# A gated unit on one core: the first half's down products as seven block products, with the weight combinations made during its up products

## The chip, the cores and the metric

The kernel runs on one core of a Trainium2 chip. The time of an execution is the device time of that core in microseconds (us). TensorE is called PE here, VectorE DVE, ScalarE ACT, GpSimd POOL; SP is the engine that issues most transfers.

## What is computed

The input x has 2048 tokens of 640 features. Two blocks follow one another, each with a layer norm that is shifted and scaled by values made from c (adaLN), and a residual. The first block is a state-space convolution over the tokens, made with Fourier transforms. The second is a bilinear gated unit with 1536 hidden features:

```python
h = _layernorm(x) * (1 + cb) + sb
g = h @ w_gate                  # 2048 x 640 by 640 x 1536
u = h @ w_up
y = (g * u) @ w_down            # 2048 x 1536 by 1536 x 640
x = x + gb * y
```

All is in float32. Each matrix product is made as three: every operand is split into a high part, rounded to the type that PE takes, and the rest, the low part; then high by high, low by high and high by low are added.

## The kernel before

The convolution takes the first 500 us and the change does not touch it. The gated unit works on two halves of the tokens. A half is two blocks of 512 tokens, T = 0 and 1, held with the features on the partitions. The hidden features are 12 groups of 128 (NF = 12); f counts them within a half, i = 12 * half + f over both.

**Gate and up products.** They are made as seven block products over the two token blocks and combinations of the weights. `x_1` and `x_2` make one of the seven, from the split gate weights `WS[i]` that `split_g` prepares; for f from 2 to 8 they run three groups ahead. `y_1`, `z_1`, `y_2`, `z_2`, `y_3` add the other six in two banks of PSUM. Between them ACT and DVE read a bank (`s`, `z`), and DVE multiplies at the end of `y_3`: `h` and `a` are the products of gate and up for the two blocks. A bank that is read in the middle goes on being added to: `y_3` must wait until DVE has read `z`. `sums_u` makes sums of raw weights, `split_u` splits them. All products of the two halves' x, y and z have 512 columns.

**Down products, second half.** `down` makes them as seven block products (Winograd's form of Strassen's scheme), over two halves of the hidden features and two halves of the 640 output columns (DC = 320). Product j runs over six chunks c; m = 6j + c counts the 42 chunks. `d_sum` makes the sums of activations, `d_prep` splits them into `AH[m]`, five chunks ahead. The weight combinations lie, already split, in the DRAM tensor `wdc`; `w_load(q)` brings chunks 2q and 2q + 1 of it through POOL's queue into one of four `wsg` buffers, so that load q waits for the chunks of load q - 4. `post` adds finished products to the residual rows. Products 0, 2, 4, 6 add up in four banks (`ACC["A"]`), products 1 and then 3, 5 in four others (`ACC["C"]`).

**The weight combinations.** `fold` scales the rows of the down weights by gb on POOL and writes them to the DRAM tensor `wdg`, during the first half's up products. During the second half's up products, at steps listed in `FOLD`, `f_load` reads a third of it, `f_sum` makes four sums on DVE, `f_hi` the seven high parts on ACT and `f_lo` the seven low parts on DVE, and both write them to `wdc`.

**Down products, first half.** `plain` makes them for one token block after the other without block products: 12 groups, four rows of 128 tokens, three products, each row of 640 columns in pieces of 384 and 256. `p_prep` splits activations and weights, the latter from `wdg`. Between its groups `LATER` puts the preparation of the second half.

**Order.** It is written out by hand: what the program calls first stands first in an engine's queue, and every engine works its queue in order. Split gate weights are kept in the DRAM tensor `wsd` for the second half.

Of the kernel before, what the change touches and what calls it, by code (L numbers as in the profile page):

```python
# [224 lines left out]
def tile_kernel(ctx: ExitStack, tc: tile.TileContext, I, out):  # L225
# [768 lines left out]
    PAIRS = [("g", 2 * p) for p in range(NF // 2)] + [("d", T, 2 * p) for T in range(2) for p in range(NF // 2)]  # L994
    NP = len(PAIRS)

    def raw():

        t = mk(f"wga{(NP - len(PAIRS)) % 2}", [P, 2 * D])
        k = PAIRS.pop(0)  # L1000
        f = k[-1]
        if k[0] == "g":
            t = t.rearrange("p (k m) -> p k m", k=NB)
            SY.dma_start(t, wv[0][:, :, f * P : f * P + 2 * P])
            w = [t[:, :, j * P : j * P + P] for j in range(2)]
        else:
            t = t.rearrange("p (k m) -> p k m", k=2)
            SY.dma_start(t, wdg[:, f : f + 2, :])
            w = [t[:, j] for j in range(2)]
        for j in range(2):  # L1010
            WR[(*k[:-1], f + j)] = w[j]

    def used(f):
        if f % 2 and PAIRS:
            raw()
# [15 lines left out]
    def split_g(i):  # L1031
        t = wsg()
        WS[i] = tuple(t[:, j].rearrange("p (k m) -> p k m", k=NB) for j in range(2))
        if i >= NF:
            G.dma_start(t, wsd[:, i - NF])
# [72 lines left out]
    def x_1(i):  # L1108
        UX[i] = UA[i] = pa(i % 5)
        prod(UX[i], [(WS[i], k, HX[0], k) for k in (0, 1)], last=False)  # L1110
        x_e(i)
# [217 lines left out]
    for t in range(3 * NK + 24):  # L1329
# [17 lines left out]
        if t == 3 * NK + 1:  # L1347
# [5 lines left out]
            wdg = dram1.tile([P, NF, D], F32, name="wdg")  # L1353
            wsd = dram1.tile([P, NF, 2, D], F32, name="wsd")
# [115 lines left out]
    AP, WD2, AC, BP = {}, {}, {}, {}  # L1470

    def p_prep(tb, f):
        w = WR.pop(("d", tb, f))
        t = wsg()
        WD2[tb, f] = t[:, 0], t[:, 1]
        m = tb * NF + f
        if m < 2:
            AP[tb, f] = tuple(mk("e", [P, 512], F32, 4).bitcast(F32R) for _ in range(2))
        else:
            if m in (2, 21):  # L1480
                n, k = ((SX, 9), (H2, 3))[m > 2]
                BP[0] = tuple(mk(x, [P, k, 512], F32R) for x in n)
            AP[tb, f] = tuple(h[:, (m - 2) % 9 if m < 21 else m - 21] for h in BP[0])
        hilo(*AP[tb, f], AT[NF * tb + f])
        hilo(*WD2[tb, f], w)
        used(f)

    C0 = 384

    def plain(tb, f):  # L1490
        if f == 0:
            b = [pa(j) for j in (2, 3, 4, 0, 1, 5)]
            c1 = [b[j].rearrange("p (t d) -> p t d", t=2)[:, :, : D - C0] for j in (2, 5)]
            AC[tb] = [(b[j][:, :C0], c1[t // 2][:, t % 2]) for t, j in enumerate((0, 1, 3, 4))]
        (ah, al), (dh, dl) = AP.pop((tb, f)), WD2.pop((tb, f))
        for t in range(4):
            ts = slice(t * P, t * P + P)
            for n, (x, w) in enumerate(((ah, dh), (al, dh), (ah, dl))):
                for c in range(2):
                    cs = slice(0, C0) if c == 0 else slice(C0, D)  # L1500
                    st = f == 0 and n == 0 and (c == 0 or t % 2 == 0)
                    PE.matmul(AC[tb][t][c], x[:, ts], w[:, cs], start=st, stop=f == NF - 1 and n == 2 and (c == 0 or t % 2 == 1))  # L1502

    XR = {}

    def res_l(tb, b):
        XR[tb] = mk(f"xb{b}", [P, 4, D])
        SY.dma_start(XR[tb], x2d[:, 4 * tb : 4 * tb + 4, :])

    def fin(tb):  # L1510
        for t in range(4):
            x = XR[tb][:, t, :]
            V.tensor_tensor(x[:, :C0], AC[tb][t][0], x[:, :C0], op=OP.add)
            V.tensor_tensor(x[:, C0:], AC[tb][t][1], x[:, C0:], op=OP.add)
            SY.dma_start(outv[:, 4 * tb + t, :], x)

# [26 lines left out]
    def down(half, m, last=False):  # L1543
        j, c = divmod(m, NH)
        if c == 0:
            if j == 0:
                ACC["A"] = [pa(t) for t in range(4)]
            if j in (1, 3):
                ACC["C"] = [pa(4), pa(5), pg(), pg()]
        ps = ACC["AC"[j in (1, 3, 5)]]  # L1550
        w = [WD[m // 2][:, l, c % 2 * DC : c % 2 * DC + DC] for l in range(2)]
        for t in range(4) if not last else (last - 1,):
            for n, (a, b) in enumerate(((0, 0), (1, 0), (0, 1))):
                PE.matmul(ps[t][:, :DC], AH[m][a][:, t * P : t * P + P], w[b], start=c == 0 and n == 0 and j in (0, 1, 3), stop=c == NH - 1 and n == 2, skip_group_check=True)  # L1554
# [8 lines left out]
    def post(half, j, ts=range(4), E=None):  # L1563
# [4 lines left out]
        for t in ts:  # L1568
            V.tensor_tensor(x[:, t], ps[t][:, :DC], x[:, t], op=OP.add)
# [12 lines left out]
    def tokens2(tb, T, k, dve):  # L1582

        tv = a_tile((TV0, TV1)[T] + k)
        head_t(pg() if tb > 1 else pa((0, 1, 4, 5)[k % 4]), tv, k, XB[tb][:, :, k * P : k * P + P], dve)
# [11 lines left out]
    def fold(f):  # L1597

        r, p = divmod(f - 1, 3)
        if f > 9:  # L1600
            if f == 10:
                head_l(2)
            return
        if f and p == 0:
            FT[9] = mk("xb0", [P, 4, D])
            SY.dma_start(FT[9], wv[2][:, 4 * r : 4 * r + 4, :])
        elif f:
            for k in range(2 * p - 2, 2 * p):
                G.tensor_tensor(FT[9][:, k], FT[9][:, k], gbr, op=OP.mult)
            if p == 2:  # L1610
                SY.dma_start(wdg[:, 4 * r : 4 * r + 4, :], FT[9])
# [33 lines left out]
    FOLD = {n: [] for n in range(80)}  # L1645
    for r in range(3):
        b = (1, 13, 25)[r]
        for n in range(4):
            FOLD[b + 1 + n // 2].append((f_sum, n))
        for j in range(7):  # L1650
            o = b + 3 + j + (max(j - 1, 0) if r == 2 else 0)
            FOLD[o].append((f_hi, r, j, j))
            FOLD[o + 1].insert(0, (f_lo, r, j))
        if r < 2:
            FOLD[b + 10].append((f_load, r + 1))

    def combos(n):
        for g_, *a_ in FOLD.get(n, ()):
            g_(*a_)

    SUMS = [(0, 4), (1, 0), (1, 1), (1, 2), (0, 5)] + [(1, c) for c in range(3, NH)] + [(2, c) for c in range(NH)]
    LATER = {(0, 1): [(stats, 2, 0)], (0, 2): [(stats, 2, 2)], (0, 3): [(head_i, 2, (0, 1))], (0, 4): [(head_i, 2, (2, 3))],
             (0, 6): [(raw_u, NF)], (0, 9): [(raw_u, NF + 1)], (1, 0): [(new_h,), (tokens2, 2, 0, 0, False)], (1, 1): [(head_l, 3), (tokens2, 2, 0, 2, False)],
             (1, 2): [(sums_u, NF), (tokens2, 2, 0, 1, False)], (1, 3): [(split_u, NF), (tokens2, 2, 0, 3, False)],
             (1, 4): [(tokens2, 2, 0, 4, False), (stats, 3, 0), (sums_u, NF + 1)], (1, 5): [(stats, 3, 2), (res_l, 1, 0)],
             (1, 6): [(head_i, 3, (0, 1))], (1, 7): [(head_i, 3, (2, 3))],
# [200 lines left out]
```

## Time and profile before

| | |
|---|---|
| Time, median of 3 runs | 987.37 us (986.79 to 993.78) |
| Profiled execution: time, span | 988.54 us, 986.8 us |
| PE busy | 889.2 us, 90% of the span |
| DVE, ACT, POOL busy | 723.8, 579.4, 509.1 us |
| Mean granted PE clock | 0.961 |
| First half's gate and up products | about 527 to 670 us |
| First half's down products | 670 to 759 us |
| Second half's gate and up products | 759 to 908 us |
| Second half's down products, end | 908 to 987 us |

The span runs from the first to the last recorded instruction; the time holds 1.7 us more. Times within the profile count from the start of the span. In a row of a timeline stand start and duration in us, the engine, the line of the kernel, the operation, its output and inputs, and in brackets how long the engine was idle before it and for what it waited. In a row of a group stand the count, the total in us and the mean in ns.

### The profile page before, as it was taken

To read this page: it belongs to the slowest core of one execution; us is meant where nothing else is said; L and a number is where in the kernel's file an instruction comes from. 1 tells how busy PE (TensorE), PEld (TensorE's weight loads), DVE (VectorE), ACT (ScalarE), POOL (GpSimd) and SP (SyncE) were. 2 spreads that over 40 slices of the span, in tenths; PEclk is the share of its full clock that TensorE was granted. 3 is DMA by queue.
4 is the path that set the end of the run, shared out by engine and by line. 5 is a ranking of instruction groups with operands and counts; after the bars stand their busy time and mean duration, and the time that the engine had idled before them with its cause. 6 is when DMAs were issued, how large, how long until landed. Compare 5 with 4: busy or idle time off the path is not lost.

```text
span 986.8 us, 26765 instructions
## 1 busy us (share of the span) xinstructions
PE 889.2 (90%) x11134; PEld 720.2 (73%) x11134; DVE 723.8 (73%) x1400; ACT 579.4 (59%) x1076; POOL 509.1 (52%) x400
## 2 busy tenths in 40 slices
PE   4867898799789789988879999999999999999998
PEld 3565556586476557667736888889999788888998
DVE  8789568888978888794857665457676756578952
ACT  4869989987888887863336333334355443435430
POOL 5978899699879979960030354440113122222110
PEclk9877979999989889999999999999999999999999
DMA  7746654556246534658595665733564676658875
GB/s 254 262 142 223 204 194 147 172 165 185 77 153 181 152 105 126 205 172 257 189 273 191 222 191 182 242 125 113 184 217 124 197 231 222 222 179 292 237 244 187
DMA packets 158817, 188.54 MB, mean 191 GB/s; under 512 B 9828, under 2 KB 128360, under 8 KB 157544
## 3 DMA queue, kind: packets, MB, share of 16 engines
q1 hardware_dynamic: 149480, 155.51, 49.4%
q0 software_dynamic: 4752, 21.63, 7.6%
q10 hardware_dynamic: 4464, 9.70, 2.6%
q8 instruction: 87, 1.43, 0.6%
q14 instruction: 34, 0.28, 0.1%
HBM read 124.22 MB, written 62.59 MB: 189 GB/s over the span
## 4 chain that ended last, share of the span: by engine, by line
PE 55%; DVE 14%; ACT 12%; issue 10%; POOL 4%; DMA 3%; SPq 0%; DVEq 0%; POOLq 0%; ACTq 0%
PE pa L1078 18%; PE psg L1078 9%; PE pa L1502 9%; PE psfc L893 2%; PE kg L826 2%; PE kg L811 2%; PE psfa L893 2%; PE psfb L893 2%; ACT trb L230 1%; ACT tra L230 1%; PE psfc L950 1%; POOL EQ L714 1%; PE psfb L950 1%; PE pa L1554 1%; ACT L230 1%
## 5 line engine op out<-in xcount | busy, mean ns | idle before, releaser
L1055 POOL TENSOR_TENSOR tf<-wur,wgb 128x256 f32<-128x256 f32 x23 | 17.8, 775 | 246.9 <-DVE wtl L1026 199.5
L714 POOL TENSOR_TENSOR EQ<-LQ,RH 128x1536 f32<-128x1536 f32 x40 | 124.1, 3104 | 9.7 <-DVE QtB L771 9.5
L1026 DVE TENSOR_TENSOR wtl<-tf,wth 128x256 fp32r<-128x256 f32 (+1 forms) x72 | 36.7, 513 | 59.7 <-ACT wth L230 59.7
L714 POOL TENSOR_TENSOR Phb<-LH,DH 128x1536 int32<-128x1536 int32 x20 | 62.2, 3112 | 13.9 <-ACT tra L230 13.9
L714 POOL TENSOR_TENSOR EP<-LP,RH 128x768 f32<-128x768 f32 x40 | 66.0, 1650 | 0.0
L714 POOL TENSOR_TENSOR Pha<-LH,DH 128x1536 int32<-128x1536 int32 (+1 forms) x21 | 62.4, 2971 | 2.3 <-ACT trb L230 2.0
L1502 PE MATMUL pa<-wsg,sh 128*128 128x384 f32 (+1 forms) x304 | 58.4, 311 | 0.0
L826 PE MATMUL kg<-QtB,PtB 64*32 64x64 f32 x2560 | 48.7, 229 | 5.8 <-DVE QtB L770 5.3
L826 PEld LDWEIGHTS kg<-QtB,PtB 64*32 64x32 f32 x2560 | 41.7, 114 | 16.1 <-issue 7.2
L1502 PEld LDWEIGHTS pa<-wsg,sh 128*128 128x128 f32 x304 | 45.7, 189 | 0.0
L1541 POOL DMA_DIRECT2D wsg<-wdc x21 | 11.2, 531 | 66.5 <-PE pa L1554 35.6
L1026 DVE TENSOR_TENSOR wsg<-wga,wsg 128x640 fp32r<-128x640 f32 x36 | 33.7, 943 | 13.8 <-ACT wsg L230 13.8
L230 ACT ACTIVATE sh<-a 128x512 fp32r<-128x512 f32 x55 | 33.3, 625 | 13.9 <-PE psg L1554 6.2
L230 ACT ACTIVATE wsg<-wga 128x640 fp32r<-128x640 f32 x36 | 26.1, 730 | 25.0 <-PE pa L1502 12.8
L1026 DVE TENSOR_TENSOR sl<-a,sh 128x512 fp32r<-128x512 f32 x55 | 37.5, 702 | 4.0 <-ACT sh L230 4.0
L1078 PE MATMUL pa<-hh,wsg 128*128 128x512 f32 x150 | 40.2, 394 | 0.0
L1148 POOL TENSOR_SCALAR hfa<-xb,hr,hr 128x128 f32<-128x128 f32 x4 | 2.3, 577 | 67.5 <-DVE hr L283 67.5
L230 ACT ACTIVATE s<-pa 128x512 f32<-128x512 f32 x12 | 7.2, 598 | 48.5 <-PE pa L1078 48.5
L769 DVE TENSOR_TENSOR QtA<-tra,EQ 128x1024 f32<-128x1024 f32 x20 | 24.4, 1220 | 15.0 <-PE kg L811 7.0
L230 ACT ACTIVATE wth<-tf 128x256 fp32r<-128x256 f32 (+1 forms) x72 | 32.5, 481 | 4.9 <-DVE tf L1056 1.8
L230 ACT ACTIVATE a<-pa 128x512 f32<-128x512 f32 x12 | 7.2, 598 | 47.7 <-PE pa L1078 47.7
L1502 PE MATMUL pa<-wsg,sl 128*128 128x384 f32 (+1 forms) x152 | 34.4, 308 | 0.0
(656 smaller groups left out, 3125.6 us busy)
## 6 DMA issues: line engine op xcount, KB each, us to landing
wsg<-wdc POOLq DMA_DIRECT2D x21, 640.0 KB, 5.3
wgb<-B_w_gate SPq DMA_DIRECT2D x24, 320.0 KB, 4.6
wur<-B_w_up SPq DMA_DIRECT2D x24, 320.0 KB, 5.8
wsd<-wsg SPq DMA_DIRECT2D x12, 640.0 KB, 3.9
wga<-wdg SPq DMA_DIRECT2D x12, 640.0 KB, 3.9
wsg<-wsd POOLq DMA_DIRECT2D x12, 640.0 KB, 4.9
wdc<-xb SPq DMA_DIRECT2D x21, 320.0 KB, 3.3
TVb<-WD SPq DMA_DIRECT2D x22, 256.0 KB, 3.5
```

Of the source, the lines that this page charges most:

```text
L230: return S.activation(o, i, f, **kw)
L714: G.tensor_tensor(o.rearrange("p x (h l) -> p x h l", l=8), lo.unsqueeze(2).to_broadcast([P, rows, nh, 8]), hi.rearrange("p h x -> p x h") ...
L769: return [lambda: V.tensor_tensor(Qt[:, :, :, 0:32], tr[:, :, :, ::-1], e[:, :, 0:32].unsqueeze(1).to_broadcast([P, 2, R, 32]), op=OP.mult ...
L811: PE.matmul(kg[j * 32 : j * 32 + 32, dd, :], PtA[:, c, dl * 4 + j, :], QtA[:, c, dl * 4 + j, :], start=dd == 0 and c == 0, stop=False, til ...
L826: PE.matmul(kg[j * 32 : j * 32 + 32, dd, :], PtB[lo : lo + 64, c, r, :], QtB[lo : lo + 64, c, r, :], start=False, stop=dd == 7 and c == 1, ...
L893: PE.matmul(r[c][par * 64 : par * 64 + 64, i, :], t_tw[:, k0 + k, c, :], src[:, k, :], start=True, stop=True, tile_position=(0, par * 64))
L950: PE.matmul(r[par][:, i], t_ti[lo : lo + 64, qd * 4 + i, c, :], x[lo : lo + 64, c, i, :], start=c == 0, stop=c == 1, tile_position=(lo, 0))
L1026: V.tensor_tensor(lo, v, hi, op=OP.subtract)
L1055: E.tensor_tensor(t[:, 0:2], u[:, 0:2], g[:, 0:2], op=OP.subtract)
L1078: PE.matmul(ps, w[a][:, k], x[b][:, l], start=first and n == 0 and m == 0, stop=n == 2 and m == len(ks) - 1, skip_group_check=True)
L1502: PE.matmul(AC[tb][t][c], x[:, ts], w[:, cs], start=st, stop=f == NF - 1 and n == 2 and (c == 0 or t % 2 == 1))
L1541: G.dma_start(WD[q], wdc[:, q // 3, q % 3])
```

## The change

The first half's down products are made by `down`, `d_sum`, `d_prep`, `w_load` and `post`, as the second half's. `plain`, `p_prep`, `fin`, `fold`, the tensor `wdg` and `LATER` are gone. `f_load` now reads the down weights themselves and `f_gb` scales them, on POOL or DVE; this and the sums, splits and writes to `wdc` stand in the first half's steps, which `PLAN` lists. Its numbers count 3f, 3f + 1 and 3f + 2 for the three places of group f, and 36 + m for chunk m of the first half's down products. The second half's `FOLD` steps are gone. In the first half `d_sum` runs on POOL, in the second on DVE as before.

So that one bank is free for transposes, the first half's `ACC["C"]` uses three banks from product 3 on: the fourth row of tokens goes into the rests of two of them, in pieces of 192 and 128 columns. Only gate groups 0 to 3 are kept in `wsd`; 4 to 11 are loaded and split again in the second half. `SU` says for which groups `sums_u` runs on POOL; the others go to DVE.

```diff
-    PAIRS = [("g", 2 * p) for p in range(NF // 2)] + [("d", T, 2 * p) for T in range(2) for p in range(NF // 2)]
+    PAIRS = [2 * p for p in range(NF // 2)] + [2 * p for p in range(NF // 2 + 2, NF)]
...
     def split_g(i):
         t = wsg()
         WS[i] = tuple(t[:, j].rearrange("p (k m) -> p k m", k=NB) for j in range(2))
-        if i >= NF:
+        if NF <= i < NF + 4:
             G.dma_start(t, wsd[:, i - NF])
             return
         hilo(*WS[i], WR.pop(("g", i)))
         if i > 3:
-            keep(i, t)
             used(i)
...
     def down(half, m, last=False):
         j, c = divmod(m, NH)
         if c == 0:
             if j == 0:
-                ACC["A"] = [pa(t) for t in range(4)]
+                ACC["A"] = [[(pa(t), 0, 0, DC)] for t in ((0, 2, 3, 1), (1, 2, 3, 0))[half]]
             if j in (1, 3):
-                ACC["C"] = [pa(4), pa(5), pg(), pg()]
+                b = [pa(4), pg(), pg()]
+                ACC["C"] = [[(x, 0, 0, DC)] for x in b]
+                if half == 0 and j == 3:
+                    ACC["C"].append([(b[0], DC, 0, 512 - DC), (b[1], DC, 512 - DC, DC)])
+                else:
+                    ACC["C"].insert(1, [(pa(5), 0, 0, DC)])
         for t in range(4) if not last else (last - 1,):
             for n, (a, b) in enumerate(((0, 0), (1, 0), (0, 1))):
-                PE.matmul(ps[t][:, :DC], AH[m][a][:, t * P : t * P + P], w[b], ...
+                for x, o, c0, c1 in ps[t]:
+                    PE.matmul(x[:, o : o + c1 - c0], AH[m][a][:, t * P : t * P + P], w[b][:, c0:c1], ...
...
-            SY.dma_start(FT["f"][:, 2 * j : 2 * j + 2], wdg[:, 2 * r + NH * j : 2 * r + NH * j + 2, :])
+            SY.dma_start(FT["f"][:, 2 * j : 2 * j + 2], wv[2][:, 2 * r + NH * j : 2 * r + NH * j + 2, :])
+
+    def f_gb(n, E=None):
+        (E or G).tensor_tensor(FT["f"][:, n], FT["f"][:, n], gbr, op=OP.mult)
...
+    SU = ((0, 1, 2, 3, 6, 8, 10, 11), (2, 5, 6, 7, 9, 10, 11))
+    PLAN = {
+        4: [(f_gb, 1, V), (f_gb, 2), (f_gb, 3, V)],
...
+        27: [(f_load, 2), (d_sum, 0, 0), (d_sum, 0, 1)],
+        28: [(raw_u, NF), (f_gb, 0)],
...
+        36: [(d_sum, 0, 3), (xq_l, 0, 0, 0, 0), (f_hi, 2, 4, 4), (f_lo, 2, 3)],
...
+        40: [(d_sum, 1, 4), (d_sum, 1, 0), (new_x, 3), (d_sum, 1, 1), (row_l, 2, 1), (d_sum, 2, 0), (d_sum, 1, 3)],
+        41: [(d_sum, 2, 2), (d_sum, 2, 1)],
...
     def combos(n):
-        for g_, *a_ in FOLD.get(n, ()):
+        for g_, *a_ in PLAN.get(n, ()):
             g_(*a_)
...
             if f + 2 < NF:
-                sums_u(i + 2)
+                sums_u(i + 2, (V, G)[f in SU[half]])
...
-            if todo and m > 0:
+            if half and todo and m > 0:
                 d_sum(*todo.pop(0), V)
-            if j < 6:
+            if j < 6 or half == 0:
                 down(half, m)
...
+            if half == 0:
+                combos(36 + m)
+        if half == 0:
+            post(0, 6)
+            continue
```

Two pieces of the queues show what was moved. The first is DVE's, in the first half's last groups. Before, from its reading `s` of group 10 to its reading `z` of group 11 (L1441 and L1449 are the reads of `z_2` and `y_3`, L1451 is `a`, L1026 a low part):

```order
L1441 TENSOR_TENSOR a_8743<-psg,a_8743 128x512
L1449 TENSOR_TENSOR a_8797<-pa_8478,z 128x512
L1451 TENSOR_TENSOR a_8545<-a_8545,a_8743 128x512
L1026 TENSOR_TENSOR e<-a_7629,e 128x512
L1026 TENSOR_TENSOR wsg<-wga_8524,wsg 128x640
L1436 TENSOR_TENSOR z<-pa_8579,z 128x512
```

The same stretch now, with the lines of the changed kernel (L1554 is a weight sum, L1566 a low part of a combination, L1017 any other low part):

```order
L1430 TENSOR_TENSOR a_8815<-psg,a_8815 128x512
L1554 TENSOR_TENSOR xb_8741<-xb_8741 128x2x320
L1566 TENSOR_TENSOR xb_8741<-xb_8741,xb_8742 128x2x320
L1554 TENSOR_TENSOR xb_8742<-xb_8741 128x640
L1017 TENSOR_TENSOR hl_8746<-a_7628,hl_8746 128x512
L1438 TENSOR_TENSOR a_8886<-pa_8516,z 128x512
L1440 TENSOR_TENSOR a_8586<-a_8586,a_8815 128x512
L1554 TENSOR_TENSOR xb_8742<-xb_8741,xb_8742 128x640
L1566 TENSOR_TENSOR xb_8741<-xb_8741,hst 128x2x320
L1017 TENSOR_TENSOR hl_8746<-a_7629,hl_8746 128x512
L1566 TENSOR_TENSOR xb_8742<-xb_8742 128x640
L1425 TENSOR_TENSOR z<-pa_8623,z 128x512
```

Between the two reads there were four instructions; now there are ten, six of them for the weight combinations. Three gains and another sum stand just ahead of this piece, after group 9's `a`.

The second piece is POOL's, in the first half's down products. Before, POOL issued there only the loads of kept gate weights for the second half, with the second half's first token sums (L1403, L1404):

```order
L1035 DMA wsg<-wsd 128x1280
L1403 TENSOR_TENSOR a_9754<-a_9341,a_9698 128x512
L1404 TENSOR_TENSOR a_9755<-a_9381,a_9753 128x512
L1035 DMA wsg<-wsd 128x1280
L1403 TENSOR_TENSOR a_9795<-a_9426,a_9738 128x512
L1404 TENSOR_TENSOR a_9796<-a_9478,a_9794 128x512
```

Now, from the third activation sum behind the load for chunks 8 and 9 to the load for chunks 12 and 13 (L1483 is `w_load`, L1474 to L1479 are `d_sum`):

```order
L1474 TENSOR_TENSOR hh_8745<-a_8292,a_8886 128x512
L1475 TENSOR_TENSOR a_8292<-a_7632,a_8292 128x512
L1477 TENSOR_TENSOR a_7630<-hh_8745,a_7630 128x512
L1483 DMA wsg<-wdc 128x1280
L1477 TENSOR_TENSOR a_7632<-hh_8745,a_7632 128x512
L1477 TENSOR_TENSOR a_7628<-hh_8745,a_7628 128x512
L1477 TENSOR_TENSOR a_7629<-hh_8745,a_7629 128x512
L1479 TENSOR_TENSOR a_8155<-a_8155,a_7628 128x512
L1477 TENSOR_TENSOR a_7631<-hh_8745,a_7631 128x512
L1479 TENSOR_TENSOR a_8375<-a_8375,a_7630 128x512
L1479 TENSOR_TENSOR a_8267<-a_8267,a_7629 128x512
L1483 DMA wsg<-wdc 128x1280
```

Two sums stand ahead of the first row shown, behind the load before. Every load of the down stage is now in one queue with these sums, and each is issued only when those ahead of it are done.

More of the change, by code (lines that the diff above doesn't have):

```diff
@@ L1468, in d_pair @@
         return tuple(h[:, l % 9] for h in AR[l > 8])
[L1470 to L1515, printed above, removed]
     def d_prep(m):
@@ L1735, in tile_kernel @@
             split_u(2, "a")
-            fold(1)
             z_1(1)
```

192 lines of the change are left out of this document (97 added, 95 removed).

## The prediction

> **What bounds the kernel now.** I read the page's 40 slices first, then busy time by stage, then the timelines of TensorE (PE), POOL and DVE at the places the change touches. The slices show PE at 9 or more from slice 22 to the end, at a granted clock of 9 tenths or more. The windows cut that part into its four stages: first half's gate and up products, first half's down products, second half's gate and up products, second half's down products.
>
> ```profile
> PE   4867898799789789988879999999999999999998
> core 0: us, PE busy (x) PEld busy (x) DVE busy (x) ACT busy (x) POOL busy (x), PEclk, DMA share, GB/s
> 527.00:670.00 143.00, 143.00 (x628) 117.40 (x627) 86.59 (x150) 57.37 (x123) 52.81 (x52) 1.00 0.58 193
> 670.00:759.00 89.00, 89.00 (x616) 88.74 (x615) 61.47 (x136) 46.00 (x76) 14.21 (x15) 1.00 0.47 150
> 759.00:908.00 149.00, 148.60 (x649) 121.27 (x649) 100.32 (x169) 61.63 (x126) 39.56 (x54) 1.00 0.69 226
> 908.00:987.00 79.00, 74.73 (x507) 74.15 (x505) 50.84 (x91) 22.68 (x39) 8.99 (x17) 0.99 0.72 222
> ```
>
> PE is busy for all of the first two windows at clock 1.00, while DVE has 56 and 28 us free there, ACT more. So this part's length is PE's work plus what PE waits. PE's pace is read from starts, since the spans of pipelined matmuls overlap.
>
> ```profile
> 643.51 0.61 PE L1078 MATMUL pa<-sh,wth 128*128 128x512 f32 x2
> 652.35 0.61 PE L1078 MATMUL pa<-sh,wth 128*128 128x512 f32 x2
> 670.03 7.20 PE L1502 MATMUL pa<-wsg,e 128*128 128x384 f32 x48
> 677.07 0.46 PE L1502 MATMUL pa<-wsg,sh 128*128 128x384 f32 x2
> 715.79 0.60 PE L1169 MATMUL psg<-ident,xb 128*128 128x128 f32 x4
> 716.15 0.54 PE L1502 MATMUL pa<-wsg,sh 128*128 128x384 f32 x2
> 908.36 1.48 PE L1554 MATMUL pa<-wsg,hl 128*128 128x320 f32 x9
> 912.44 0.53 POOL L1541 DMA_DIRECT2D wsg<-wdc  x1 [11.71 <-PE pa L1554]
> 915.97 0.53 POOL L1541 DMA_DIRECT2D wsg<-wdc  x1 [3.00 <-PE pa L1554]
> 919.49 0.53 POOL L1541 DMA_DIRECT2D wsg<-wdc  x1 [3.00 <-PE pa L1554]
> ```
>
> The first two rows stand one late group f apart: 39 matmuls of 512 columns in 8.84 us, 226.7 ns each. The plain down products take 7.04 us for 48, 146.7 ns each (24 of 384 columns, 24 of 256). In the second half each load of a pair of down weights is released by 24 matmuls of 320 columns, and comes every 3.52 us: 146.7 ns each, 1.76 us a chunk of 12. Four transposes of 128 columns take 0.36 us, 90 ns each.
>
> **The change, part by part.** *Fewer matmuls.* Before: 2 blocks x 12 groups x 4 rows of tokens x 3 x 2 column pieces = 576 in the first half's down stage. After: 7 products x 6 chunks x 4 x 3 = 504, of which 36 (the fourth row of tokens in products 3 and 5) are cut into pieces of 192 and 128 columns: 468 of 320 columns and 72 short ones. Before 576 x 0.1467 = 84.5 us; now 468 x 0.1467 = 68.7 us and 36 pairs. A line through 512 and 320 columns (80.0 ns for 192) gives 93 ns for 192 columns and 67 for 128, so 0.160 us a pair is the least; two full 0.1467 are the most, 0.293. The transposes at 90 ns are the nearest row to the 128 piece, so I take 0.093 + 0.090 = 0.183, 6.6 us in all (5.8 to 10.6). The gain on PE is 84.5 - 68.7 - 6.6 = **9.2 us** (5.2 to 10.0). The 40 transposes, the gate and up products and all ahead of them stay.
>
> *Work that lies beside PE.* Gone from DVE and ACT: 24 splits of down weights (820 ns on DVE below) and 24 of activations; from SP and POOL the copies of gate weights 4 to 11 through wsd, and the scaled weights through wdg. New in the first half: 42 splits, and the weight combinations. These are 12 sums (L1618) and 21 low parts (L1630) on DVE, their 21 high parts on ACT; half of POOL's 12 gains go to DVE.
>
> ```profile
> L1630 DVE TENSOR_TENSOR xb<-xb 128x640 fp32r<-128x640 f32 x9 | 8.5, 948 | 0.0
> L1618 DVE TENSOR_TENSOR xb<-xb 128x640 f32<-128x640 f32 x9 | 8.0, 884 | 0.2
> L1026 DVE TENSOR_TENSOR sl<-a,sh 128x512 fp32r<-128x512 f32 x55 | 37.5, 702 | 4.0 <-ACT sh L230 4.0
> 672.04 0.82 DVE L1026 TENSOR_TENSOR wsg<-wga,wsg 128x640 fp32r<-128x640 f32 x1
> 672.77 0.69 DVE L1026 TENSOR_TENSOR sl<-a,sh 128x512 fp32r<-128x512 f32 x1
> 673.37 0.82 DVE L1026 TENSOR_TENSOR wsg<-wga,wsg 128x640 fp32r<-128x640 f32 x1
> ```
>
> About 37 us more for DVE in the first up stage (33 x 0.9, six gains at 0.8, four groups of sums from POOL, less what spills into the down stage) makes some 124 of 143: hidden on the whole. The second half loses those 33 instructions and gets 8 gate splits, so its cover grows. I cost both stages at nothing but for two places where an order is too tight; without that cover each microsecond would count in full.
>
> *Place 1, groups 9 to 11 of the first half.* These have no gate products left and last 8.84 us. PE may start the last products (y_3) of group 11 only when DVE has read its bank (z). Between DVE's two products of group 9 and that z now stand 10 instructions of 640 columns (3 gains, 4 sums, 3 low parts), 7 of 512 and group 11's split of up weights. By starts: 10 x 0.73 + 7 x 0.61 + 2.0 (split, from the rows below) = 13.6 us. PE leaves 6.80 of group 11 and 8.84 of group 10, less 1.42 for the two products: 14.2 us. It fits by 0.6, if nothing stretches it. But POOL now makes a gain and two sums at that time.
>
> ```profile
> 648.04 0.43 DVE L1026 TENSOR_TENSOR wtl<-tf,wth 128x256 fp32r<-128x256 f32 x1 [1.80 <-ACT wth L230]
> 649.08 0.42 DVE L1026 TENSOR_TENSOR wtl<-tf,wth 128x256 fp32r<-128x256 f32 x1
> 650.68 0.69 DVE L1441 TENSOR_TENSOR s<-psg,s 128x512 f32<-128x512 f32 x1
> 751.13 1.28 POOL L1404 TENSOR_TENSOR a<-a,a 128x512 f32<-128x512 f32 x1 [1.36 <-DVE a L1402]
> 752.94 1.30 POOL L1403 TENSOR_TENSOR a<-a,a 128x512 f32<-128x512 f32 x1
> 752.89 1.90 DVE L1401 TENSOR_TENSOR a<-a,a 128x512 f32<-128x512 f32 x1 [1.85 <-ACT a L230]
> 754.83 0.69 DVE L1402 TENSOR_TENSOR a<-a,a 128x512 f32<-128x512 f32 x1
> 752.35 0.57 POOL L1035 DMA_DIRECT2D wsg<-wsd  x1
> L1403 POOL TENSOR_TENSOR a<-a,a 128x512 f32<-128x512 f32 x2 | 2.6, 1294 | 1.1 <-ACT a L230 1.1
> 590.11 1.46 POOL L1055 TENSOR_TENSOR tf<-wur,wgb 128x256 f32<-128x256 f32 x1 [5.47 <-DVE wtl L1026]
> 578.53 1.20 POOL L1056 TENSOR_TENSOR tf<-wur,tf 128x256 f32<-128x256 f32 x1
> 602.50 0.73 POOL L1055 TENSOR_TENSOR tf<-wur,wgb 128x256 f32<-128x256 f32 x1 [8.72 <-DVE wtl L1026]
> L1058 POOL TENSOR_TENSOR tf<-wgb,tf x23: 732/743/1329, 517.6 to 890.9; 128x256 f32<-128x256 f32 x23
> ```
>
> A DVE instruction with both operands in SBUF takes 0.69 us alone, 1.90 when it starts with one of POOL's: it waits for POOL's 1.30. The other way, POOL's 0.73 becomes 1.20 or 1.46. Three such waits of 1.2 us, less 0.6, are **3.0 us** for PE. The least is 0 (POOL falls in gaps), the most 5 (all 4.2 us of POOL, and the last down rows come late: the load of 2 x 640 KB stands on SP behind the writes of the combinations before it). If z is late, h of group 11 and so the start of the down stage are late by as much.
>
> *Place 2, POOL's queue in the down stage.* In the second half DVE makes the 24 activation sums and POOL only issues loads. In the first half POOL does both, in one order. Count from PE's first down matmul, T. The load for chunks 8 and 9 goes out at T + 4.1 (912.44 - 908.36), when chunk 1 has freed its buffer. Behind it now stand 5 sums, the load for chunks 10 and 11, 7 sums, and only then the load for chunks 12 and 13, which in the second half goes out at T + 11.1.
>
> ```profile
> wsg<-wdc POOLq DMA_DIRECT2D x21, 640.0 KB, 5.3
> DMA to landing us min/median/max: 4.1/5.3/7.9
> ```
>
> PE wants it at T + 12 x 1.76 = T + 21.1. Alone, 12 sums of 1.29 us bring it out at 4.1 + 0.53 + 5 x 1.29 + 0.53 + 7 x 1.29 = T + 20.6 and down at T + 25.9: PE stops for 4.8 us. It would need 0.89 us a sum to be in time. In those 16 us DVE has ten splits of chunks and low parts to make, all with two operands in SBUF, so the engines take turns. Eleven turns of 0.5 us (1.20 for 0.73) bring it out at T + 26.1, down at T + 31.4, and PE stops **10.3 us**. Bounds: 12 sums at 1.22 (751.13 to the next POOL start at 752.35), no turns, landing 4.1: 2.8. Stretched by 0.72 (1.46 for 0.74), landing 7.9: 15.4. I take the median landing and the smaller of the two stretches shown. Later loads have few sums ahead of them.
>
> The Trainium skill, SBUF — State Buffer, section Who interferes with whom, states that a DVE instruction with two SBUF inputs and a GpSimd one that reads SBUF exclude each other, and that the second "fully blocks". The rows above agree for DVE (1.90 for 0.69). By that rule POOL would lose a whole 0.69 at each of eleven turns, 2.1 us more: an estimate of 12.4 us for the stop. No run shown has such turns in a long row.
>
> *The sum.* -9.2 + 3.0 + 10.3 = +4.1 us. On the profiled execution (span 986.8, time 988.5) that is 992.6. It lay 1.2 us above the median of the runs, 987.4, so on that median **991.5 us**.
>
> **The rivals.** *POOL and DVE keep out of each other's way.* For it: half of the 23 sums in the row of L1058 took 0.743 us or less, with 0.732 the least. Then place 1 costs nothing and place 2 4.8: 987.4 - 9.2 + 4.8 = 983.0. Against it: DVE is nearly without gaps there.
>
> *Neither place binds:* the load lands before chunk 12. Then 987.4 - 9.2 = 978.2, or 977.4 with the shortest pairs. It needs sums of 0.89 us, and the rows of that shape show 1.28 to 1.30.
>
> *Slower by over 1%: turns at every instruction.* Place 2 at 15.4, place 1 at 5: 987.4 - 9.2 + 20.4 = 998.6. It decides from 19.1 us of waits on, such as the load for chunk 12 issued after T + 30 with place 1 at its worst. For it: 1.90 for 0.69 means that DVE's own splits, one in 1.9 us, fall behind PE's chunk of 1.76. Against it: DVE has a head start of five chunks, and beside the 0.72 that POOL lost at 590.11 stand 0.47 at 578.53.
>
> *The change doesn't buy what it counts:* short pieces cost as much as full ones. Then the gain is 5.2 and the time 995.5.
>
> **How the numbers follow.** Forecast 0.50, both apart 0.20, neither binds 0.10, turns everywhere 0.15, dear pieces 0.05. A measurement of this kernel tells about 1% (9.9 us) from no change. Faster by that (below 977.5) is only a part of the third case, with the shortest pairs, or with a gain that I have not seen: 0.06. Slower (above 997.2): most of the fourth case, and the upper ends of the forecast and of the fifth: 0.21. Within 1%: 0.73. The forecast's own range is 985 to 998. The least of both places (0 and 2.8) with the longest gain gives 980.2, so the range of 8 in 10 begins just below, at 979.5; it goes to 1000, a little beyond the fourth case.
>
> **What would show it.** Right: in the first half's down stage L1554's successor runs in 540 matmuls with 146 ns between starts; one wait of PE near chunk 12, put down to the DMA wsg<-wdc, of 8 to 12 us, with POOL without gaps before it and rows of POOL sums between 1.3 and 2.0; a wait of some 3 us of PE for DVE's z at the end of the first up stage. Wrong: no wait at chunk 12; POOL's sums well below 1.2; pairs at other than 0.18; waits of PE in the second half; or a load that misses chunk 10 already, which would put the loss two chunks earlier.

## The result and the profile after

| | before | after |
|---|---|---|
| Time, median (runs) | 986.87 us (985.22 to 993.78, 6) | 1001.75 us (993.68 to 1006.48, 6) |
| Profiled execution: time, span | 988.54, 986.8 us | 1001.87, 1000.1 us |
| First half's gate and up products | 144.7 us | 156.2 us |
| First half's down products | 89.1 us | 90.0 us |
| Second half's gate and up products | 149.2 us | 148.2 us |
| Second half's down products, to the last matmul's start | 74.7 us | 75.2 us |

The change makes the kernel slower by 1.3%: the ratio is 1.0129, with a 95% interval of 1.0096 to 1.0162. On the median of before that is 999.6 us, where I had said 991.5: the range, which goes to 1000, holds it only at its very end. The stages are counted between starts of PE's matmuls, from the first `x_1` at its full width (525.37 us before, 526.75 after): so 1.4 of the 13.3 us of span lie ahead of them, in the convolution. That start lay between 520.1 and 526.8 in the profiled executions below, so the argument goes by the stages behind it.

Nearly all of the loss is in the first up stage, 11.5 us. The down stage, with 8 us less of matmuls, takes 0.9 us more. Busy time by stage, after:

```profile
core 0: us, PE busy (x) PEld busy (x) DVE busy (x) ACT busy (x) POOL busy (x), PEclk, DMA share, GB/s
528.60:682.90 154.30, 147.22 (x627) 118.94 (x625) 129.05 (x202) 70.22 (x142) 50.77 (x46) 0.98 0.60 199
682.90:772.90 90.00, 83.28 (x582) 82.77 (x581) 77.99 (x148) 39.77 (x67) 40.18 (x42) 0.96 0.77 239
772.90:921.10 148.20, 148.20 (x650) 121.47 (x649) 88.83 (x167) 56.53 (x120) 22.38 (x28) 1.00 0.33 101
921.10:1000.00 78.90, 74.40 (x505) 73.86 (x503) 48.27 (x87) 19.89 (x34) 9.00 (x17) 1.00 0.63 192
```

PE now stands still 7.1 us in the first stage and 6.7 in the second, and its clock is below 1.00 in both. DVE is at 84 and 87%. PE's largest waits in the gated unit (total, times, longest; the last, 1.1 us, lies at the end of the second half, where the kernel before waits 0.7):

```profile
PE pa L1502 <- DVE sl L1017: 6.7, 1, 6.7
PE pa L1068 <- DVE z L1425: 4.4, 3, 3.6
PE psg L1068 <- ACT z L230: 2.4, 1, 2.4
PE pa L1502 <- DMA wsg<-wdc: 1.1, 1, 1.1
```

**Place 2, the down stage.** The stop is at chunk 9 and not at 12, and its releaser is DVE's low part `sl`, not the load. The timeline there:

```profile
694.80 13.25 DVE L1017 TENSOR_TENSOR sl<-a,sh 128x512 fp32r<-128x512 f32 x4
695.97 0.57 POOL L1483 DMA_DIRECT2D wsg<-wdc  x1
696.56 3.76 POOL L1477 TENSOR_TENSOR a<-hh,a 128x512 f32<-128x512 f32 x3
700.28 1.26 POOL L1479 TENSOR_TENSOR a<-a,a 128x512 f32<-128x512 f32 x1
701.50 1.26 POOL L1477 TENSOR_TENSOR a<-hh,a 128x512 f32<-128x512 f32 x1
702.72 2.48 POOL L1479 TENSOR_TENSOR a<-a,a 128x512 f32<-128x512 f32 x2
705.15 0.57 POOL L1483 DMA_DIRECT2D wsg<-wdc  x1
705.80 0.63 PE L1502 MATMUL pa<-wsg,sl 128*128 128x320 f32 x1 [6.72 <-DVE sl L1017]
```

POOL runs seven sums from 696.56 to 705.15, 1.23 us each, with nothing between them. DVE's four splits, 0.68 us each alone, take 13.25 from 694.80 on; the longest of them takes 9.25, as the row of these splits says (least, median and longest, in ns):

```profile
L1017 DVE TENSOR_TENSOR sl<-a,sh x11: 667/683/9247, 684.9 to 715.6; 128x512 fp32r<-128x512 f32 x11
```

So there are no turns here: POOL has its access for the whole row, and DVE none. The load for chunks 12 and 13 goes out at T + 22.2 (705.15 - 682.93), but PE is late already. Without the stop PE would have wanted it at T + 21.1, and no such load in this run landed in under 4.0 us: by this estimate a wait of some 5 us at chunk 12, where I had predicted 10.3, lies hidden behind the stop at chunk 9.

**Place 1, the end of the up stage.** Two stops, both by DVE beside POOL:

```profile
654.97 1.83 POOL L1547 TENSOR_TENSOR xb<-xb,gbr 128x640 f32<-128x640 f32 x1 [1.49 <-DVE wtl L1017]
655.40 1.67 DVE L1046 TENSOR_TENSOR tf<-wur,tf 128x256 f32<-128x256 f32 x1
657.00 2.13 DVE L1047 TENSOR_TENSOR tf<-wur 128x256 f32<-128x256 f32 x1
659.06 1.50 DVE L1048 TENSOR_TENSOR tf<-wgb,tf 128x256 f32<-128x256 f32 x1
662.50 1.65 PE L1068 MATMUL psg<-sh,wsuh 128*128 128x512 f32 x3 [2.43 <-ACT z L230]
663.95 1.48 PE L1068 MATMUL psg<-sh,wsul 128*128 128x512 f32 x3
674.41 2.35 DVE L1017 TENSOR_TENSOR hl<-a,hl 128x512 fp32r<-128x512 f32 x1
676.68 1.88 DVE L1566 TENSOR_TENSOR xb<-xb 128x640 fp32r<-128x640 f32 x1
679.23 1.22 PE L1068 MATMUL pa<-hh,wth 128*128 128x512 f32 x2 [3.61 <-DVE z L1425]
```

In group 9 three sums of weights, 0.42 us each alone, take 5.3 us beside POOL's gain and sums. The row of the second of them over the whole run, as above:

```profile
L1047 DVE TENSOR_TENSOR tf<-wur x10: 409/418/2134, 546.3 to 891.6; 128x256 f32<-128x256 f32 x10
```

With them the products of group 9 are late, and ACT can write the one buffer `z` of group 10 only behind them: 2.43 us. Later the low parts ahead of group 11's `z` take 2.35 and 1.88 us for 0.68 and 0.82: 3.61 us.

**Each stop costs more than its length.** Behind the 6.72 us, PE's first 15 matmuls start 0.275 us apart, then 0.147:

```profile
700.00:705.00 5.00, 0.00 (x0) 0.00 (x0) 5.00 (x1) 2.30 (x4) 5.00 (x5) 0.80 0.61 228
705.00:708.00 3.00, 2.20 (x8) 2.20 (x9) 3.00 (x4) 0.00 (x0) 2.81 (x4) 0.50 0.53 119
711.00:715.00 4.00, 4.00 (x29) 4.00 (x29) 4.00 (x11) 0.58 (x2) 0.98 (x2) 1.00 0.69 190
```

The granted clock is 0.50 from 705 to 708 and 1.00 from 711 on; PE's slow start costs 709.93 - 705.80 - 15 x 0.147 = 1.9 us more. The three matmuls that start at 662.50 above, after a stop of only 2.43 us, take 0.48 us each for 0.227 (663.95 - 662.50). The two stops of place 1 cost 1.7 us more each in this way. The Trainium skill, TensorE: Matmul & The Clock Gate, Part 1, states half rate after an idle window of about 3.4 us. The stop of 6.72 us agrees; that of 2.43 is shorter than the page's window, and PE ran at half pace all the same. So it did after a stop of 2.79 us in the seventh kernel below, there from 1.2 us after the stop: 0.267 us a matmul for 0.147.

### The profile page after: what moved, and what is told of

The parts are those of the page before. It is cut to its first block, busy times and chain, and to the rows that moved or that the text cites. A ratio compares the mean times of both kernels' runs of the same rounds, so it can differ in the third digit from the quotient of the medians.

```text
span 1000.1 us, 26719 instructions
## 1 busy us (share of the span) xinstructions
PE 889.8 (89%) x11098; PEld 720.2 (72%) x11098; DVE 769.3 (77%) x1458; ACT 578.3 (58%) x1078; POOL 515.9 (52%) x395
## 5 line engine op out<-in xcount | busy, mean ns | idle before, releaser
L1045 POOL TENSOR_TENSOR tf<-wur,wgb 128x256 f32<-128x256 f32 x14 | 13.6, 974 | 186.6 <-DVE wtl L1017 178.8
L1483 POOL DMA_DIRECT2D wsg<-wdc x42 | 22.8, 545 | 122.6 <-PE pa L1502 66.4
L1017 DVE TENSOR_TENSOR wtl<-tf,wth 128x256 fp32r<-128x256 f32 (+1 forms) x72 | 38.3, 533 | 47.9 <-ACT wth L230 47.9
L1502 PE MATMUL pa<-wsg,sh 128*128 128x320 f32 (+1 forms) x272 | 69.2, 313 | 0.0
L1017 DVE TENSOR_TENSOR sl<-a,sh 128x512 fp32r<-128x512 f32 x56 | 49.9, 920 | 2.2 <-ACT sh L230 2.2
L1502 PEld LDWEIGHTS pa<-wsg,sh 128*128 128x128 f32 x272 | 48.6, 191 | 0.0
L1502 PE MATMUL pa<-wsg,sl 128*128 128x320 f32 (+1 forms) x136 | 42.6, 313 | 6.7 <-DVE sl L1017 6.7
L1502 PE MATMUL psg<-wsg,sh 128*128 128x320 f32 x168 | 43.1, 303 | 0.0
L1518 DVE TENSOR_TENSOR wga<-pa,wga 128x320 f32<-128x320 f32 (+1 forms) x44 | 19.2, 478 | 27.4 <-PE pa L1502 27.4
```

What stands on the lines that cost most here:

```text
L1017: V.tensor_tensor(lo, v, hi, op=OP.subtract)
L1045: E.tensor_tensor(t[:, 0:2], u[:, 0:2], g[:, 0:2], op=OP.subtract)
L1483: G.dma_start(WD[q], wdc[:, q // 3, q % 3])
L1502: PE.matmul(x[:, o : o + c1 - c0], AH[m][a][:, t * P : t * P + P], w[b][:, c0:c1], start=c == 0 and n == 0 and j in (0, 1, 3) and o == 0, ...
L1518: V.tensor_tensor(x[:, t, c0:c1], b[:, o : o + c1 - c0], x[:, t, c0:c1], op=OP.add)
```

## The experiments

My theory after the comparison: DVE is late at both places because its instructions with two operands in SBUF are kept out by POOL's (the clash), and PE restarts slowly. Rivals: DVE has too much to do there; POOL's queue delays the loads, as I had predicted; and, later, the third load of raw down weights comes too late. Stage lengths are of the profiled executions, from the same starts as above.

| kernel | time, ratio to before (95%) | up 1 | down 1 | down 2 |
|---|---|---|---|---|
| 1 sums on DVE | 989.4, 1.0020 (0.9994 to 1.0045) | 149.9 | 86.0 | 74.6 |
| 2 sums spread | 996.8, 1.0088 (1.0073 to 1.0104) | 155.7 | 92.3 | 74.6 |
| 3 place 1 on DVE | 999.5, 1.0110 (1.0087 to 1.0133) | 155.6 | 90.8 | 75.1 |
| 4 before, sums on POOL | 995.1, 1.0076 (1.0056 to 1.0095) | 144.7 | 89.1 | 83.4 |
| 5 combinations early | 997.1, 1.0116 (1.0074 to 1.0158) | 152.7 | 88.7 | 75.0 |
| 6 early, sums on DVE | 984.8, 0.9981 (0.9958 to 1.0004) | 149.1 | 84.2 | 75.3 |
| 7 before, sums on POOL, spread | 994.3, 1.0075 (1.0048 to 1.0102) | 144.7 | 89.1 | 80.5 |
| 8 still earlier, rows early | 988.9, 1.0019 (0.9996 to 1.0042) | 154.6 | 82.2 | 75.2 |
| 9 one load one step earlier | 981.4, 0.9944 (0.9925 to 0.9962) | 148.4 | 81.0 | 75.2 |
| 10 rows early alone | 983.2, 0.9957 (0.9935 to 0.9979) | 149.4 | 84.9 | 74.3 |
| 11 before, dependent rows | 996.8, 1.0089 (1.0056 to 1.0121) | 144.7 | 89.1 | 85.2 |
| 12 the ninth, sums on POOL | 995.5, 1.0064 (1.0042 to 1.0087) | 154.8 | 90.1 | 75.1 |

**1. The sums on DVE.**

```diff
-    def d_sum(j, c, E=G):
+    def d_sum(j, c, E=V):
```

> The changed kernel with the first half's 36 activation sums (d_sum) on DVE in place of POOL; nothing else moves. Theory (clash): DVE is late at both places since its instructions with two SBUF operands stand locked out while POOL works; without POOL's sums both stops of PE (2.4 + 3.6 us at the end of the up stage, 6.7 us at chunk 9) and their slow restarts go, about 18 us: 980 to 985 us. Rival (DVE has too much to do there): DVE gets 24.8 us more of work (36 x 0.69), the stops stay or grow: 1001 to 1012 us. Rival (POOL's queue delays the loads of down weights): the stop at chunk 9 goes, those of the up stage stay: 991 to 994 us.

989.4 us, 12.4 less than the changed kernel, though DVE got 25 us more of work. The stop at chunk 9 is gone, and 6.3 us of the up stage. That refutes "too much work" as the main cause. But 4 to 9 us of what I expected are missing: a stop of 2.4 us for `z` stays, and in the down stage DVE stands 3.8 us for rows of x ahead of the statistics, with splits queued behind.

**2. The sums of the down stage spread.**

```diff
-        38: [(d_sum, 0, 5), ...], 39: [..., (d_sum, 0, 4), (d_sum, 1, 2)], 40: [(d_sum, 1, 4), (d_sum, 1, 0), ...
+        38: [(d_sum, 0, 4), ...], 40: [(d_sum, 1, 0), (d_sum, 0, 5), ...], 42: [(d_sum, 1, 1), (d_sum, 1, 2)], 44: [...
```

> The changed kernel with the sums of products 1 and 2 on POOL as before, but in other places: never more than two in a row, with a load of down weights (which waits for PE) between them. Only the down stage can change. Theory (a row of POOL instructions without waits of their own locks a DVE instruction out for the whole row): the 9.2 us instruction of DVE becomes 2 to 3 us, the stop of 6.7 us at chunk 9 and its restart go: 991 to 995 us, with both stops at the end of the up stage as they were. Rival (DVE has too much to do): DVE does the same work, the stop stays: 999 to 1002 us. Rival (the loads): no stop for a DMA in either, no statement on the split.

The long instruction is gone, but the stage is 92.3 us, 2.4 longer, and the time met neither range. PE's largest wait there:

```profile
PE pa L1502 <- DVE sl L1017: 5.1, 8, 1.3
```

One stop became eight. So the length of the row is not what costs here; the sums of POOL take time from DVE, which has little to spare in this stage, in short rows too. (The median is 5.0 us lower all the same. The profiled execution was 6.6 us ahead at the first `x_1` already, where the code is the same, so the median doesn't speak for the edit.)

**3. Place 1 alone on DVE.**

```diff
-        27: [(f_load, 2), (d_sum, 0, 0), (d_sum, 0, 1)],
-        28: [(raw_u, NF), (f_gb, 0)],
+        27: [(f_load, 2), (d_sum, 0, 0, V), (d_sum, 0, 1, V)],
+        28: [(raw_u, NF), (f_gb, 0, V)],
```

and `(d_sum, 0, 2, V)` at step 31.

> The changed kernel with the gain and the six sum instructions that POOL has in groups 9 to 11 of the first half on DVE; the down stage is as it was. Theory (clash): DVE gets 5 us more of work but none of it beside POOL; the stops of 2.4 and 3.6 us and their restarts go or shrink to 1 us: 990 to 994 us, with the stop at chunk 9 left. Rival (DVE has too much to do in groups 9 to 11): 13.6 us of work in a room of 14.2 become 14.8 and the products of group 9 come 3 us later: the stops grow, 1003 to 1007 us.

The time lies in neither range, and the up stage hardly changed: 155.6 us, where the second kernel, with the same code there as the changed one, has 155.7. The timeline shows why my edit didn't test what it should:

```profile
656.64 0.83 DVE L1547 TENSOR_TENSOR xb<-xb,gbr 128x640 f32<-128x640 f32 x1 [3.49 <-issue]
701.47 0.39 PE L1502 MATMUL pa<-wsg,sh 128*128 128x320 f32 x1 [2.71 <-DMA wsg<-wdc]
```

DVE now stands 3.49 us ahead of the first gain. The profile names no releaser, but the gain needs only the third load of raw weights, which was issued from 647.4 to 648.9; such loads take 6.3 to 7.4 us to land in this run. That points to a second cause at place 1: in the changed kernel this load goes out at 650.2, so the third set's gains, sums and low parts are squeezed into the time from 655 to group 11's `z` at 678.5. The second row: the load for chunks 10 and 11 comes late here, the loss "two chunks earlier" of my prediction.

**4. The old kernel with the suspected cost.** Its second half gets the sums on POOL in the changed kernel's bunches; DVE has less to do.

```diff
-            if todo and m > 0:
-                d_sum(*todo.pop(0), V)
+            for s in BUNCH.get(m, ()):   # 2: (0,5)  3: (0,4) (1,2)  4: (1,4) (1,0) (1,1) (2,0) (1,3)  5: (2,2) (2,1) ...
+                d_sum(*s)
```

> The kernel before, with the sums of the second half's down stage on POOL in the same bunches as the changed kernel has in its first half (eight in a row ahead of the load for chunks 12 and 13); nothing else. DVE has less to do. Theory (clash): a DVE split is locked out for the row of sums, up to 9 us, but DVE comes into this stage with less behind it than in the changed kernel: a stop of PE of 2 to 7 us around chunks 9 to 12, with its restart 990 to 996 us. Rival (POOL's queue delays the load, as I predicted for the changed kernel): PE waits about 5 to 10 us for the DMA at chunk 12, 992 to 998 us. Rival (DVE has too much to do): nothing or a gain, 984 to 988 us.

```profile
920.73 10.96 DVE L1026 TENSOR_TENSOR sl<-a,sh 128x512 fp32r<-128x512 f32 x2
922.49 3.76 POOL L1535 TENSOR_TENSOR a<-hh,a 128x512 f32<-128x512 f32 x3
931.09 0.57 POOL L1541 DMA_DIRECT2D wsg<-wdc  x1
931.75 0.64 PE L1554 MATMUL pa<-wsg,sl 128*128 128x320 f32 x1 [6.64 <-DVE sl L1026]
```

The same stop at the same chunk, 6.6 us, in a stage that had no stop above 0.7 us, and the stage is 8.7 us longer: the stop, some 1.7 of restart (13 matmuls from 931.75 to 935.35), and a few tenths. This one edit makes place 2's loss.

**5 and 6. Combinations early; then the sums on DVE too.**

```diff
-        24: [(f_lo, 1, 4), (f_lo, 1, 3), (f_hi, 1, 5, 5)], ... 27: [(f_load, 2), ...]
+        21: [(f_lo, 1, 4), (f_lo, 1, 3), (f_hi, 1, 5, 5)], ... 24: [(f_load, 2)],
```

The sixth has also `E=V` in `d_sum`, and the statistics of the fourth token block one and two chunks later.

> The changed kernel with the second and third set of weight combinations three to four steps earlier, so that the third load of raw down weights (which landed 6 us before DVE needed it in group 9) and its gains and sums come a group sooner; activation sums on POOL as they were. Theory (the end of the up stage has two causes, the clash with POOL and the late third load that bunches 13.6 us of DVE work into 14.2 us): the stops of 2.4 and 3.6 us shrink to 2 us together, the up stage from 156.2 to 147 to 151 us, the down stage stays: 993 to 997 us. Rival (the clash alone): the sums of POOL still stand beside DVE's products, the up stage stays above 153 us: 998 to 1002 us.

> The last kernel with, besides, all activation sums of the first half on DVE, and the statistics of the fourth token block one and two chunks later in the queue (DVE stood 3.8 us before them for rows of x). Theory (the loss is DVE's lateness at the two places, made by the clash and the late load): the up stage is within 2 us of its length before the change (144.7), the down stage within 3 of 79.9: 979 to 984 us, faster than before. Rival (DVE is full in the first 30 us of the down stage even without POOL): the down stage stays at 85 to 87 us: 985 to 989 us, no faster than before.

The early load takes 3.5 us from the up stage (156.2 to 152.7), less than I expected: two causes, and the clash is the larger. They don't add up: the sixth, with both, takes 7.1 us from that stage, where the first had 6.3 alone. Between the fifth and the sixth lie 12.3 us, as 12.4 lay between the changed kernel and the first, though here the statistics have moved too. The sixth is not distinguishable from the kernel before, 0.8 us above my range; among what it lacks to my 979 to 984 are transposes that now wait 2.7 us for ACT, behind the later statistics.

**7. The old kernel, one sum to a chunk.** As the fourth, but `d_sum(*todo.pop(0), G)` in the old places.

> The kernel before with the sums of the second half's down stage on POOL, but one to a chunk as they stood on DVE, so that a load which waits for PE stands behind every second one; to be held against the kernel with eight in a row, which lost 8.7 us in that stage. Theory (a DVE instruction is locked out for a row of POOL instructions, and a short row costs little where DVE has time left): no stop above 1 us, 987 to 990 us. Rival (each sum on POOL costs DVE its own length wherever it stands): the stop stays, 992 to 996 us. Rival (the loads come late behind the sums): PE waits for the DMA wsg<-wdc.

```profile
912.11 3.40 DVE L1630 TENSOR_TENSOR xb<-xb 128x640 fp32r<-128x640 f32 x1
912.26 2.56 POOL L1535 TENSOR_TENSOR a<-hh,a 128x512 f32<-128x512 f32 x2
915.43 5.16 DVE L1026 TENSOR_TENSOR sl<-a,sh 128x512 fp32r<-128x512 f32 x2
917.02 1.31 POOL L1532 TENSOR_TENSOR s<-a,a 128x512 f32<-128x512 f32 x1
918.41 1.64 POOL L1533 TENSOR_TENSOR a<-a,a 128x512 f32<-128x512 f32 x1
```

Here DVE pays a row of two: 3.40 us for 0.82, and 0.82 + 2.56 = 3.38. The stage is 5.7 us longer with two stops of 3.3 together. The theory's range failed, and the time and the stop are the first rival's: each sum costs DVE about its own length here too. Short rows cost somewhat less than the long one (8.7), but far from nothing.

**8, 9 and 10. Towards a faster version.** The eighth moves both later sets one more step and the rows of x (`row_l`) of the fourth block from chunks 12 to 14 to 10 and 11; the ninth only the third load and its gains and sums, with the rows; the tenth only the rows. All three put the statistics back in their place. The lines are the ninth's against the sixth.

```diff
-        22: [(f_hi, 1, 6, 6), (f_lo, 1, 5)], 23: [(f_lo, 1, 6)], 24: [(f_load, 2)], 26: [(f_gb, 0)], ...
+        22: [(f_lo, 1, 5), (f_hi, 1, 6, 6), (f_lo, 1, 6)], 23: [(f_load, 2)], 25: [(f_gb, 0)], ...
-        48: [(row_l, 3, 1)], 49: [(row_l, 3, 0)], 50: [(row_l, 3, 2), (row_l, 3, 3)],
+        46: [(row_l, 2, 0), (row_l, 3, 1)], 47: [(row_l, 3, 0), (row_l, 3, 2), (row_l, 3, 3), ...],
```

> The last version of the changed kernel (all activation sums of the first half on DVE, weight combinations early) with the second and third set of combinations one more step earlier, and the rows of x of the fourth token block asked for ahead of the first finished products, since SP's queue held them for 15 us behind a write of the output that waited for DVE; the statistics go back to their place. If the loss is DVE's lateness alone: the up stage within 2 us of its length before (144.7), the down stage at 81 to 83, 979 to 982 us, faster than before by 0.5 to 0.8%. If something else holds the gain back (the short pieces, which take 0.22 us a pair, or DVE full without POOL): 984 to 987 us, the same as before.

> As the kernel with sums on DVE and combinations early (up stage 149.1, down stage 84.2), the second set left in its place, only the third load of raw down weights one step earlier, so that its gains and first sums fall where DVE stood idle 5 us of 10; and the rows of the fourth token block asked for early, as in the last kernel (down stage 82.2). Theory (DVE bunched): up stage 145 to 147.5, down 82 to 82.5, 978.5 to 981.5 us, faster than before by 0.6 to 0.9%. Rival (DVE is full in sum from group 8 on, wherever the load stands): up stage stays at 149, 982 to 983.5 us.

> As the kernel with sums on DVE and combinations early, with only the rows of the fourth token block asked for early and the statistics back in their place. The up stage stays at 149.1; the down stage goes from 84.2 to 82.2 as in the last kernel: 982 to 984 us, 0.3 to 0.5% faster than before. Rival (the gain of the rows belonged to the other changes): 984 to 986 us.

The eighth failed in the up stage: PE stops for DVE's `z` and ACT's `s` from 603 on already (1.2, 0.9 and 1.6 us) and for 2.5 at the end. DVE is busy 19.8 of 20 us from 602 on, but it was so in the sixth without a stop; which instruction tips it stays open. The ninth has the lowest median of all, 0.56% below before (0.38 to 0.75), though not clear of the tenth's 0.43% (0.21 to 0.65). Its up stage, 148.4, is 1 us above my range, as the rival would have it. Its first up and down stage:

```profile
523.60:670.10 146.50, 144.57 (x626) 116.61 (x625) 124.24 (x211) 68.72 (x140) 36.01 (x36) 1.00 0.61 203
670.10:751.10 81.00, 81.00 (x581) 80.93 (x581) 70.21 (x165) 40.88 (x70) 17.60 (x26) 1.00 0.85 276
```

PE is without a gap for the whole down stage: 81.0 us for 89.1. This is the gain of the change undisturbed. The tenth's stage stayed at 84.9 in its profile, so the rows alone don't show the 2 us I gave them, though its median is in the range. (Its profiled execution took 986.85 us, 3.7 above that median, so this stage isn't typical of its runs.)

**11. Dependent rows.** The fourth kernel with the seven sums ahead of the load for chunks 12 and 13 in an order in which three read what the one before them wrote.

```diff
-4: [(1, 4), (1, 0), (1, 1), (2, 0), (1, 3)], 5: [(2, 2), (2, 1)], 7: [(2, 3)]
+4: [(1, 0), (2, 0), (1, 1), (2, 1), (1, 3)], 5: [(2, 3), (2, 2)], 7: [(1, 4)]
```

> The kernel before with sums on POOL in bunches (6.6 us stop of PE, 8.7 us lost in the stage), with the seven sums ahead of the load for chunks 12 and 13 in another order: three of them now read what the one just ahead of them wrote, so that POOL can't start them before that is done. All else is the same. In the traces DVE got between two POOL instructions only where the second started after the end of the first. Theory (back-to-back POOL instructions keep DVE out, a gap lets it in): DVE's 10 us instruction is cut to pieces of 3 us or less and the stop of PE to 1 to 4 us; POOL's sums behind a gap take 1.6 to 1.9 us; 989 to 993 us. Rival (DVE is kept out until POOL's queue is empty): 6 us or more of stop, 994 to 997 us.

```profile
920.78 1.63 POOL L1537 TENSOR_TENSOR a<-a,a 128x512 f32<-128x512 f32 x1
922.37 1.86 POOL L1535 TENSOR_TENSOR a<-hh,a 128x512 f32<-128x512 f32 x1
923.02 3.46 DVE L1026 TENSOR_TENSOR sl<-a,sh 128x512 fp32r<-128x512 f32 x2
924.84 0.41 PE L1554 MATMUL pa<-wsg,sl 128*128 128x320 f32 x1 [1.07 <-DVE sl L1026]
930.61 0.57 POOL L1541 DMA_DIRECT2D wsg<-wdc  x1
934.84 0.61 PE L1554 MATMUL pa<-wsg,sh 128*128 128x320 f32 x1 [6.36 <-DVE hl L1026]
```

The mechanism is as the theory says: with gaps between POOL's sums DVE gets in, its splits take 1.73 us each, POOL's sums 1.6 to 1.9, and the stop at chunk 9 shrinks from 6.6 to 1.07. My time was wrong, and fell into the rival's range for another reason than the rival's: the load for chunks 12 and 13 now goes out at T + 24.8 (930.61 - 905.85), lands 4.1 us later, at 934.7, and PE stops 6.36 us at chunk 12. (The row names DVE's `hl`, but chunk 12 is of the `sh`, `sl` pair, and the load's landing fits to 0.1 us.) This is the stop that I had predicted, in place of the other.

**12. The fastest version with the sums on POOL again.** One word, `E=G`.

> The fastest version (981.4 us, down stage 81.0, up stage 148.4) with the 36 activation sums of its first half on POOL again, one word of the code. Theory (the engine of the sums alone costs 12 us, as between the two other pairs of kernels, 12.4 and 12.3): 990 to 995 us, stops of PE for DVE's splits in the down stage and for z at the end of the up stage. Rival (the order has removed the cause): 981 to 984 us.

PE's two largest waits:

```profile
PE pa L1502 <- DVE sl L1017: 6.5, 1, 6.5
PE pa L1068 <- DVE z L1425: 6.1, 2, 5.1
```

14.1 us slower by the medians, 12 by the ratios, and both stops are back (5.1 us for `z`, 6.5 at chunk 9). In this order too the engine of the sums is worth 12 to 14 us. Over the three pairs (the changed kernel and the first, the fifth and the sixth, the twelfth and the ninth) it is 11 to 14, and 10.3, 8.1 and 15.5 us in the first up and down stage; the middle pair differs in the statistics too.

## Why the prediction was off, step by step

The kernel became slower, as forecast, but by three times the forecast's 4.1 us. The 13.3 us of span in the profiled executions are -8.1 for PE's gain, +11.5 at place 1, +9.0 at place 2 and 0.9 elsewhere (1.4 more in the convolution, 0.5 less in the second half). That the time still lies in the range is due to the range's upper end, which I had set by another case than my forecast.

*PE's gain, 9.2 us:* right in kind, 8.1 measured (the ninth kernel's down stage). The short pairs are dearer than the 0.183 I took. In the changed kernel, the fourth row of tokens of a product with short pieces:

```profile
748.74 0.25 PE L1502 MATMUL pa<-wsg,sh 128*128 128x192 f32 x1
750.72 0.25 PE L1502 MATMUL pa<-wsg,sh 128*128 128x192 f32 x1
```

These rows are one chunk apart, 1.98 us for nine full matmuls and three pairs: (1.98 - 9 x 0.1467) / 3 = 0.22 a pair. 36 of them make 7.9 us for 6.6.

*Place 1, 3.0 us:* the step that failed; the stage lost 11.5. I saw the right engines, but counted only the path to group 11's `z` and three waits of 1.2. Left out were the three weight sums of group 9, which DVE makes beside POOL's gain (5.3 us for 1.3), the way from there over ACT's single buffer `z` to PE, and that the third load goes out so late that its work can't begin earlier. By the runs, taking POOL's sums away gives back 6.3 us of the 11.5 (first kernel), the earlier order alone 3.5 (fifth), both together 7.1 (sixth). In the ninth 3.7 us are left: PE still waits 1.9 us there for `z` and `s`, in three places, and no run says what would remove the rest.

*Place 2, 10.3 us:* the size was nearly right by luck, since the carrier was wrong. The stage lost 90.0 - 81.0 = 9.0 us. I had POOL and DVE take turns, with POOL the loser and its load late at chunk 12. In the rows POOL does take turns with DVE ahead of the load for chunks 10 and 11 (its five sums take 1.7 us each, 687.50 to 695.97), but behind it POOL loses nothing while it runs back to back, and DVE is late at chunk 9. The runs show the two as faces of one clash: eleven gives the predicted one with a load at T + 24.8 (T + 26.1 predicted) and 6.4 us, four the other with 6.6. The rival "DVE's own splits, one in 1.9 us, fall behind PE's chunk" had named the carrier, and gave 998.6. That this is nearest to the 999.6 is luck: it put 15.4 us at place 2 (15.3 by its own terms) and 5 at place 1, where 9.0 and 11.5 were lost. I set the rival against DVE's head start of five chunks, which is 8.8 us; one row of seven sums is 8.6, and the turns ahead of it had used up part of the head start.

*A term that I didn't have:* the restart, 1.7 to 1.9 us for each stop, three of them.

*The rest costed at nothing:* right for the second half, 148.2 and 75.2 us. The first up stage's average spoke for cover (124 of 143 us of DVE), and hid that the work is not spread.

## What to carry to other kernels

Before work goes to an idle engine, ask whose access it takes: here a sum on POOL kept DVE waiting for 1.23 us, and on DVE itself it takes 0.69; one word was worth 11 to 14 us. Look for cover in stretches as long as the head start of the one who waits, here 9 us, not in a stage's average. Count a stop of PE at its length and a restart, here 1.7 to 1.9 us for stops of 2.4 us and more. And when a stop is gone, look for the next one behind it: here the late load stood behind the late split.

## What the runs showed of the hardware

POOL's instructions that start back to back keep a waiting DVE instruction with two SBUF operands out for the whole row: 9.25 us for 0.68 with seven, 3.40 for 0.82 with two. Where a POOL instruction reads what the one before wrote, and so starts only after its end, DVE gets between, at 1.73 us a split, and POOL's next takes 1.6 to 1.9 for 1.25. The Trainium skill, SBUF — State Buffer, Who interferes with whom, has the lock for one whole instruction; the rows show it over rows. In the seventh kernel a gap of less than 0.1 us was enough (917.02 + 1.31 against the next start at 918.41, where the second overwrites what the first read); why so little decides it stays open.
